# Early attention steps: the mask added on TensorE, the row minimum taken straight out of PSUM, and a new written order

## The chip, the cores and the metric

One core of a Trainium2 chip runs the whole program. Its engines are TensorE (PE, with its weight load PEld), VectorE (DVE), ScalarE (ACT) and GpSimd (POOL); all transfers are issued by SyncE (SP). Each engine has its own queue and takes its instructions in the order in which the program wrote them. The metric is the device time of one execution in microseconds (us).

## The reference

`q`, `k`, `v` have 2 batches, 8 heads, 768 positions and 64 values. For every position the scores are those against all positions, masked with -1e9 where the distance is 16 or more, and next to them the scores against 24 block maxima of `k` (blocks of 32), with log 32 added:

```
scores_l_m = where(|i - j| < 16, scale * q @ k.T, -1e9)
scores_s   = scale * q @ k_sum.T + log(32)
a = softmax(concat(scores_l_m, scores_s)); x = a @ concat(v, v_sum)
x = silu(x @ w_in) @ w_out            # 1536 x 512, inner 2048
out = (x @ w_a * (x @ w_b)) @ w_out2  # inner 1536
```

## The kernel before

**Attention.** A step is 64 query positions of one batch with all 8 heads; there are 24 (12 for each batch, numbered 0 to 23). Only a window of 96 keys can be unmasked for 64 queries, so a step scores 96 + 24 = 120 columns. Its operations are: `sc` (L349) eight score matmuls into two PSUM banks; `sm` (L370) four VectorE instructions, each of which reads 128 x 120 scores out of PSUM, adds the mask, writes the sum to SBUF and leaves its row extreme; `ex` (L389) the exponential on ScalarE; `rs` (L398) sums and reciprocal; `no` (L406) the scaling, on POOL or VectorE; `tr` (L410) four transposes into one bank; `pc` (L417) their copy to SBUF; `av` (L422) the product with the values; `xh`, `xl` (L438, L441) a part rounded to `fp32r` and the remainder. Steps in the set `ACTS` (19 of 24) have negated scores in SBUF, and ScalarE does their exponential in four instructions with the row extreme as bias, which also give the sums. The others (4, 7, 11, 19, 20) have one more operation, `su` (L384), which subtracts the extreme (on POOL), one exponential of 128 x 480 and one more sum on VectorE.

**Before attention** the keys of each batch are turned (`tk`), laid out as windows by ScalarE (`wk`), and reduced to block maxima by VectorE (`mk`, `sk`, `pk`); queries are turned (`tq`) and scaled by 1/8 (`bq`, L337); values are summed in blocks (`sv`, `mv`, `kv`).

**The two multiplications after it** are the bulk of TensorE's work. `m1:f` (12 matmuls) multiplies a block of 512 rows of x with column block f of `w_in`; `sg`, `gh`, `gl` apply the silu and split it; `m2:f` (12 matmuls) multiplies with row block f of `w_out`. Weights arrive as 64-bit words and are decoded: `da` on ScalarE, `du` and `dj` on VectorE, then split by `hi` (ScalarE or VectorE) and `lo` (POOL or VectorE). In the second and third rounds the decoded `w_out` is reloaded from DRAM (`RO`) and split again (`hR`, `lR`).

**The order** is written out by hand: `ORDER` (L26 to L77) is a list of words, and a loop (L875) calls the operation of each. A last letter is the engine: a ScalarE, v VectorE, p POOL. Each engine's queue is the list cut down to its own words; SP's is the list of loads (`LQ`, `LK`, `LG`, `LV`, `LI`, `LO`, `RO`) and spills (`SP`, `PV`). The list ends with `m2:25`; the rest of the program (from L878) is made by loops.

**PSUM.** Until the word `boot` six banks go round (L133) among `tq`, `tk`, `sc`, `mv`, `tr` and `av`; after it two. A user of a bank waits for the last reader of the user before it: for `sc` that is `sm`.

## Time and profile before

| | |
|---|---|
| median of 3 runs | 640.61 us (639.71 to 643.76) |
| the profiled execution | 643.56 us, its span 641.8 us |
| PE busy | 612.9 us, 95% of the span |
| DVE, ACT, POOL busy | 396.1, 299.7, 303.9 us |
| mean granted clock of TensorE | 0.989 of full speed |
| chain that ended last | PE 71%, DVE 4%, POOL 4%, issue 2% |

Busy time counts computing instructions; a matmul's end is modelled. Times in the rows are counted from the start of the span. The granted clock is that of TensorE as a share of its full speed. "Idle before" is the time in which the engine had nothing to do ahead of an instruction, and the name behind the arrow is what it waited for last.

### The profile page before, as it was taken

The page shows a single profiled execution, that of the slowest core. Times are in us where ns is not written, and L with a number is a line of the kernel's source. Part 1 is how long each engine was busy: PE and PEld are TensorE (multiplying, and loading weights), DVE is VectorE, ACT ScalarE, POOL GpSimd, SP SyncE. Part 2 cuts the span into 40 slices and gives each one's busy share as a digit, 9 for nine tenths or more (in the row PEclk, how much of TensorE's full clock was granted, in tenths as well). Part 3 has the DMA queues.
Part 4 walks back from the last instruction along what each step waited for, and adds up shares of the span by engine and source line. Part 5 has one row for each costly group of instructions (what it writes and reads, how often), then busy time and mean ns, then how long its engine had stood idle before and what let it go on. Part 6 is the DMA issues. An engine that isn't in the chain of part 4 may idle for free.

```text
span 641.8 us, 10139 instructions
## 1 busy us (share of the span) xinstructions
PE 612.9 (95%) x3632; PEld 528.8 (82%) x3632; DVE 396.1 (62%) x768; ACT 299.7 (47%) x651; POOL 303.9 (47%) x270
## 2 busy tenths in 40 slices
...
GB/s 231 204 177 258 283 249 308 154 203 103 62 46 58 59 37 146 229 221 195 165 199 189 116 49 73 191 104 225 83 213 83 229 16 97 84 182 302 142 2 132
DMA packets 90522, 97.82 MB, mean 152 GB/s; under 512 B 39000, under 2 KB 68440, under 8 KB 90472
## 3 DMA queue, kind: packets, MB, share of 16 engines
...
q8 instruction: 29, 0.48, 0.3%
q14 instruction: 21, 0.17, 0.1%
...
## 4 chain that ended last, share of the span: by engine, by line
PE 71%; DVE 4%; POOL 4%; issue 2%; ACT 0%; ACTq 0%; DVEq 0%; POOLq 0%
PE y L557 17%; PE h L524 15%; PE bankg L762 10%; PE bankh L762 10%; PE ol L808 10%; PE o L787 5%; POOL wab L645 1%; POOL ab L727 1%; PE av L428 1%; POOL w_out L501 1%; PE sc L358 1%; PE pt L414 1%; DVE yt L677 1%; DVE pts L148 0%; DVE sm L380 0%
## 5 line engine op out<-in xcount | busy, mean ns | idle before, releaser
L524 PE MATMUL h<-x,w_in 128*128 128x512 f32 (+1 forms) x612 | 143.0, 384 | 0.0
L557 PE MATMUL y<-g,w_out 128*128 128x512 f32 x576 | 141.3, 396 | 0.0
L524 PEld LDWEIGHTS h<-x,w_in 128*128 128x128 f32 x612 | 109.9, 190 | 22.3 <-issue 0.5
L557 PEld LDWEIGHTS y<-g,w_out 128*128 128x128 f32 x576 | 107.5, 189 | 23.9 <-issue 0.5
L501 POOL TENSOR_TENSOR w_out<-re_out,w_out 128x512 fp32r<-128x512 f32 x37 | 52.4, 1416 | 114.2 <-ACT w_out L146 108.0
L808 PE MATMUL ol<-w_out,plh 128*128 128x512 f32 x192 | 59.1, 389 | 0.0
L539 DVE TENSOR_TENSOR g<-h,g 128x512 fp32r<-128x512 f32 x31 | 21.4, 691 | 46.7 <-ACT g L146 46.5
L501 POOL TENSOR_TENSOR w_out<-w_out,w_out 128x512 fp32r<-128x512 f32 x23 | 32.0, 1402 | 34.1 <-ACT w_out L146 29.5
L539 POOL TENSOR_TENSOR g<-sg,g 128x512 fp32r<-128x512 f32 x17 | 24.8, 1461 | 43.7 <-DVE g L148 18.8
L727 POOL TENSOR_TENSOR ab<-sum,ab 128x384 f32<-128x384 f32 x24 | 27.9, 1171 | 32.2 <-DVE sum L724 32.1
L532 ACT ACTIVATE h<-h 128x512 f32<-128x512 f32 x31 | 18.1, 583 | 53.8 <-PE h L524 53.7
L808 PEld LDWEIGHTS ol<-w_out,plh 128*128 128x128 f32 x192 | 36.0, 188 | 7.5
L146 ACT CAST w_out<-re_out 128x512 fp32r<-128x512 f32 x38 | 23.6, 622 | 36.4 <-issue 27.5
L808 PE MATMUL ol<-w_out,pll 128*128 128x512 f32 x96 | 37.4, 389 | 0.0
L800 DVE TENSOR_TENSOR pll<-pl,plh 128x1024 fp32r<-128x1024 f32 x12 | 17.9, 1492 | 29.9 <-ACT plh L799 29.9
L787 PE MATMUL o<-w_out,p 128*128 128x512 f32 x108 | 30.7, 397 | 0.4 <-POOL w_out L501 0.2
L380 DVE CUSTOM_DVE_ANT_0 sm<-sc,mask 128x120 f32<-128x120 f32 x96 | 21.1, 276 | 15.5 <-PE sc L358 15.4
L393 ACT ACTIVATE sm<-sm,st 128x120 f32<-128x120 f32 x76 | 29.1, 390 | 1.5 <-DVE st L380 1.4
L478 DVE SCALAR_TENSOR_TENSOR w_out<-w_out,u_out 128x512 uint32<-128x512 uint32 x28 | 27.3, 974 | 3.0 <-ACT w_out L468 1.5
L762 PE MATMUL bankh<-yhT,wab 128*128 128x384 f32 x96 | 28.3, 335 | 0.7 <-DVE sum L709 0.7
L408 POOL TENSOR_TENSOR sm<-sm,st 128x480 f32<-128x480 f32 x20 | 22.6, 1136 | 11.7 <-DVE st L404 5.3
L501 POOL TENSOR_TENSOR w_in<-w_in,w_in 128x512 fp32r<-128x512 f32 x15 | 21.3, 1424 | 13.5 <-ACT w_in L146 7.9
...
## 6 DMA issues: line engine op xcount, KB each, us to landing
...
```

The source lines that it names most:

```text
L146: nc.scalar.copy(o, i)
L393: nc.scalar.activation(sm[:, pr, :], sm[:, pr, :], AF.Exp, scale=-1.0, bias=st[:, 0, pr:pr + 1], accum_out=st[:, 1, pr:pr + 1])
L408: engines[engine].tensor_tensor(sm, sm, st[:, 3, :, None].to_broadcast([P, NPR, KK]), op=ALU.mult)
L478: nc.vector.scalar_tensor_tensor(bits, bits, 3, u_t.pop((kind, f)), op0=ALU.logical_shift_left, op1=ALU.bitwise_or)
L501: engine.tensor_tensor(w[:, 1], w32_t[kind, f], w[:, 0].bitcast(F32), op=ALU.subtract)
L524: nc.tensor.matmul(h_ps[i][:, cols], win_t[f][:, a, c * P:(c + 1) * P], x_t[n][:, steps, m, c, :], start=(idx == 0), stop=(idx == 3 * NK - 1))
L539: engines[engine].tensor_tensor(g_t[i][:, 1], sg_t.pop(i), g_t[i][:, 0].bitcast(F32), op=ALU.subtract)
L557: nc.tensor.matmul(y_ps[n, c], wout_t[i][:, a, c * P:(c + 1) * P], g_t[i][:, m, :], start=(f == 0 and (a, m) == (0, 0)), stop=(f == N1 - 1 ...
L727: engines["v" if k == 6 else "p"].tensor_tensor(at, x, at, op=ALU.mult)
L762: nc.tensor.matmul((A, B)[b], weights(u, a, s, s + 1)[:, 0, c * P:(c + 1) * P], yc_t[q, y][m][:, c, :], start=(idx == 0 and not more), sto ...
L787: nc.tensor.matmul(o_ps[t], g[:, a, c:c + P], w[:, m], start=(begins and (a, m) == (0, 0)), stop=(ends and (a, m) == PARTS[-1]))
L808: nc.tensor.matmul(late_o[j], late_p[f][a][:, j * P:(j + 1) * P], wo2_t[N2 + f][:, m], start=(f == 0 and (a, m) == (0, 0)), stop=(f == N2 ...
```

## The change

Seven steps (`MASKED`: 0, 2, 3, 4, 5, 6, 8) get their mask from TensorE: two matmuls of 66 rows by 256 columns, one for each bank, put the mask into PSUM, and the score matmuls add to it. VectorE then takes the row minimum with two reductions out of PSUM, and ScalarE's four exponentials read PSUM. So the two banks are held until `ex`. All scores are negated when the queries are scaled, and the mask's sign is turned. POOL makes the two new operands at the start (`make_mask_product`). Steps 4, 7 and 19 now have their exponential with a bias on ScalarE; 10 and 21 have the other form, so `su` is left in 10, 11, 20 (POOL) and 21 (VectorE).

The list is written anew. Between the two lists the letters move: `no` on VectorE 4 to 13 of 24, `lo` 6 to 17 of 32, `gl` 11 to 17 of 28; the others change by one or two. Lines of the old and the new list that the prediction speaks of:

```diff
@@ -21,59 +21,61 @@
 WINDOW = 16
 NEG = -1.0e9
 
-ACTS = {0, 1, 2, 3, 5, 6, 8, 9, 10, 12, 13, 14, 15, 16, 17, 18, 21, 22, 23}
+ACTS = {0, 1, 2, 3, 4, 5, 6, 7, 8, 9, 12, 13, 14, 15, 16, 17, 18, 19, 22, 23}
+
+MASKED = {0, 2, 3, 4, 5, 6, 8}
 
 ORDER = """
-LQq:0:0 br:q:0:0:a LKq:0:0 LKq:0:1 tq:0:0:1 br:k:0:0:v ok:0 tq:0:0:0 br:k:0:1:v LKq:0:2 tk:0:0:0 mk:0:0:0 tk:0:1:1
-tk:0:0:1 tk:0:1:0 qz LQ:0:1 bq:0:0:1:a bq:0:0:0:a br:k:0:2:v tk:0:2:1 tq:0:1:0 mk:0:1:1 wk:0:0:0 wk:0:0:1 mk:0:1:0
-mk:0:2:1 tk:0:2:0 wk:0:1:1 tq:0:1:1 mk:0:0:1 mk:0:2:0 wk:0:1:0 bq:0:1:0:a LG:0:1 sk:0:v sv:0:1:1:p wk:0:2:0 pk:0:0:v
-wk:0:2:1 bq:0:1:1:v LG:0:2 sc:1 sm:1 pk:0:2:a LG:0:0 LI:1 LG:0:3 pk:0:1:v sc:0 sm:0 ex:1 sc:2 LI:0 sv:0:0:4:p LQ:0:2
-sc:5 sm:2 LV:0 sm:5 ex:0 LV:1 sv:0:3:4:v rs:1 ex:2 sv:0:2:1:p mv:0:0:512:4 no:1:p ex:5 rs:0 du:in:1 mv:0:1:0:1
-mv:0:2:0:1 mv:0:3:0:4 tr:1 sc:3 no:0:p rs:2 no:2:p tq:0:2:0 du:in:0 tr:0 sm:3 kv:0:0:a pc:1:a sc:4 sm:4 tq:0:2:1 su:4:p
-tr:2 PV:0:1 pc:0:v rs:5 ex:3 bq:0:2:0:a sc:7 av:0 LV:2 rs:3 sm:7 ex:4 av:1 no:3:p su:7:p bq:0:2:1:a PV:0:2 LV:3 rs:4
-pc:2:v da:in:1 tr:3 sc:6 no:5:p xh:0:a xh:1:a sm:6 xl:0 PV:0:3 LI:3 av:2 ex:7 tr:5 xl:1 rs:7 no:4:p pc:3:a sc:8 no:7:p
-sm:8 LV:4 ex:6 LV:5 LV:6 av:3 LV:7 rs:6 xh:2:a xh:3:a no:6:p pc:5:a LI:4 tr:4 pc:4:a da:in:0 xl:2 sc:9 ex:8 dj:in:1 xl:3
-sm:9 LI:2 hi:in:1:v av:5 tr:6 sc:11 lo:in:1:p av:4 xh:5:a pc:6:a tr:7 sm:11 pc:7:a rs:8 xl:5 sc:10 av:6 xh:4:a LV:8
-LQ:1:0 av:7 da:in:4 m1:1:0 su:11:p ok:1 no:8:p dj:in:0 xh:6:a du:in:4 xl:4 xh:7:a xl:7 hi:in:0:a LK:1:1 lo:in:0:p xl:6
...
-tk:1:2:0 hi:out:1:a hi:in:6:a sg:2:p wk:1:2:0 lo:out:0:p m1:3 da:out:2 lo:out:1:p lo:in:6:p m2:0 dj:out:2 wk:1:1:1
-gh:2:a gl:2:p du:in:5 LK:1:0 da:in:5 m2:1 LO:3 SP:2 hi:out:2:v sg:3:p dj:in:5 tk:1:0:0 m1:6 LO:4 hi:in:5:a LG:1:1
...
-du:out:5 sc:13 LO:8 hi:out:4:a hi:in:7:a gh:5:a lo:out:4:p sm:13 sc:14 gl:5:v SP:4 lo:in:7:p m1:8 hi:out:6:a da:in:9
-du:in:9 m1:7 sg:8:v da:out:5 dj:in:9 sm:14 LV:9 dj:out:5 sc:12 LO:7 hi:in:9:v lo:out:6:p du:in:10 ex:10 rs:10 LG:1:2
...
-da:out:11 gl:11:v LO:12 LV:15 sm:18 tr:12 LI:14 dj:out:10 du:out:11 lo:in:15:v pc:12:v sc:16 m1:12 sg:13:p hi:out:10:a
-dj:out:11 da:in:14 PV:1:2 PV:1:3 sm:16 av:12 xh:12:a LV:14 lo:out:10:p du:in:14 gh:13:a hi:out:11:v xl:12 SP:11 m2:10
...
-sc:22 yh:0:0 lR:17:p sm:22 yh:0:3 tr:16 yh:0:2 sg:21:p gh:18:v gl:18:v pc:16:v lR:19:v sc:21 m1:19 m2:16 gh:21:v gl:21:p
-RO:20 ex:20 sg:19:p RO:23 hR:18:v sm:21 av:18 xh:18:v xl:18 m2:17 lR:18:p tr:19 ex:22 gh:19:v hR:20:a pc:19:v ex:21
...
+LQq:0:0 LKq:0:0 ok:0 br:q:0:0:a LKq:0:1 tq:0:0:1 br:k:0:1:a br:k:0:0:v tk:0:0:0 tk:0:0:1 LKq:0:2 tq:0:0:0 tk:0:1:1
+mk:0:0:0 tk:0:1:0 LG:0:1 sv:0:1:1:p mk:0:1:1 bq:0:0:1:a wk:0:0:1 br:k:0:2:v tk:0:2:1 wk:0:0:0 mk:0:0:1 mk:0:1:0 mk:0:2:1
+wk:0:1:1 LQ:0:1 wk:0:1:0 qz tq:0:1:0 wk:0:2:1 bq:0:1:0:a LG:0:0 LG:0:2 LG:0:3 bq:0:0:0:v LI:1 LI:0 tk:0:2:0 LQ:0:2
+mk:0:2:0 sk:0:v tq:0:1:1 pk:0:1:p pk:0:2:a pk:0:0:v bq:0:1:1:v wk:0:2:0 sc:1 sm:1 sc:0 sm:0 LV:0 ex:1 sc:5 sc:2 sm:2
+ex:0 LV:1 sm:5 sv:0:3:4:v rs:1 ex:2 sv:0:0:4:p sv:0:2:1:p mv:0:0:512:4 mv:0:3:0:4 no:1:v ex:5 tr:1 rs:0 no:0:p
+mv:0:1:0:1 mv:0:2:0:1 kv:0:0:a PV:0:1 sc:3 tq:0:2:0 du:in:1 rs:2 no:2:v tr:0 pc:1:v sc:4 sm:3 da:in:1 bq:0:2:0:a du:in:0
+sm:4 pc:0:v ex:3 tq:0:2:1 tr:2 ex:4 sc:7 av:0 bq:0:2:1:a rs:3 rs:5 LV:2 av:1 no:3:p sm:7 PV:0:2 rs:4 no:4:p pc:2:a tr:3
+pc:3:a no:5:v xh:1:v xh:0:a sc:6 xl:0 sm:6 LV:3 xl:1 av:2 ex:7 LI:3 ex:6 tr:5 sc:8 rs:7 PV:0:3 LV:4 sm:8 rs:6 av:3
+xh:2:a LI:4 xh:3:a xl:2 no:7:p ex:8 tr:4 LV:5 LV:7 no:6:p pc:5:v da:in:0 sc:9 pc:4:a dj:in:1 xl:3 LV:6 LI:2 sm:9 tr:6
+av:5 pc:6:a hi:in:1:a lo:in:1:p sc:11 sm:11 su:11:p tr:7 av:4 xh:5:a av:6 rs:8 LO:0 xh:4:a xl:5 dj:in:0 pc:7:a LK:1:1
+av:7 da:in:4 hi:in:0:a m1:1:0 xh:7:a ex:11 xl:7 LQ:1:0 du:in:4 xh:6:v xl:4 no:8:v lo:in:0:p sc:10 ok:1 m1:0:0 rs:11 LV:8
...
+m1:3 sg:2:p hi:in:6:a lo:in:6:p SP:0 du:in:5 wk:1:2:0 lo:out:1:v da:out:2 m2:0 dj:out:2 LK:1:0 gh:2:a wk:1:1:1 du:in:8
+gl:2:p LO:3 sg:3:p SP:2 hi:out:2:a da:in:5 mk:1:2:0 lo:out:2:p dj:in:5 m2:1 gh:3:a hi:in:5:a m1:6 da:out:3 tk:1:0:0
...
+pk:1:0:v du:in:7 da:in:7 m2:3 dj:out:6 sc:13 m1:5 LV:11 LO:8 du:out:5 dj:in:7 gh:6:a gl:6:v hi:out:4:a LI:10 hi:in:7:a
+sm:13 sc:14 sg:5:v lo:in:7:v du:in:9 SP:4 gh:5:a gl:5:v lo:out:4:v hi:out:6:a m1:8 lo:out:6:p da:in:9 LO:7 sg:8:v
+da:out:5 LV:9 LV:10 dj:in:9 sm:14 m1:7 sc:12 hi:in:9:v du:in:10 LG:1:2 ex:10 rs:10 sm:12 dj:out:5 av:9 lo:in:9:p
...
+m1:12 du:out:11 sg:13:p dj:out:11 du:out:13 lo:in:15:p PV:1:2 dj:out:10 hi:out:10:a gh:13:a sc:16 sm:16 lo:out:10:p
+LV:14 LO:14 da:in:14 PV:1:3 av:12 SP:10 rs:15 xh:12:v du:in:14 LO:15 tr:13 xl:12 hi:out:11:a no:15:v sg:12:v pc:13:a
...
+bq:1:2:1:a SP:15 sg:16:p hi:out:15:v m1:18 RO:16 sg:18:v LV:18 rs:17 no:17:p lo:out:15:v RO:23 tr:17 first no:16:p m2:15
...
+tr:18 m1:21 yh:0:1 yh:0:2 pc:18:a sc:22 rs:19 gl:18:v hR:19:v yh:0:3 no:19:p m2:16 sm:22 tr:16 m1:19 sg:21:p pc:16:v
+gh:21:a sc:21 hR:17:a lR:17:p RO:18 m2:17 LV:19 sg:19:p gl:21:p hR:23:a sm:21 su:21:v ex:20 av:18 hR:18:a lR:18:v
...
 """
 
 
@@ -147,6 +149,9 @@
         else:
             engines[engine].tensor_copy(o, i)
 
+    def ap_of(t, offset, dims):
+        return bass.AP(tensor=t.tensor, offset=t.offset + offset, ap=[list(t.ap[0])] + dims)
+
 
     ident = const.tile([P, P], F32, name="ident")
     mask = ap1.tile([P, 3, KK], F32, name="mask")
@@ -165,16 +170,16 @@
     def make_constants():
 
         nc.gpsimd.memset(mask[:, :, 0:KL], 0.0)
-        nc.gpsimd.memset(mask[:, :, KL:KK], math.log(BLOCK))
+        nc.gpsimd.memset(mask[:, :, KL:KK], -math.log(BLOCK))
         for hp in range(2):
             m = mask[hp * QS:(hp + 1) * QS, :, 0:KL]
 
-            nc.gpsimd.affine_select(out=m, in_=m, compare_op=ALU.is_ge, fill=NEG, base=-1,
+            nc.gpsimd.affine_select(out=m, in_=m, compare_op=ALU.is_ge, fill=-NEG, base=-1,
                                     pattern=[[0, 3], [1, KL]], channel_multiplier=-1)
-            nc.gpsimd.affine_select(out=m, in_=m, compare_op=ALU.is_ge, fill=NEG, base=2 * WINDOW - 1,
+            nc.gpsimd.affine_select(out=m, in_=m, compare_op=ALU.is_ge, fill=-NEG, base=2 * WINDOW - 1,
                                     pattern=[[0, 3], [-1, KL]], channel_multiplier=1)
-        nc.gpsimd.memset(mask[:, 0, 0:WINDOW], NEG)
-        nc.gpsimd.memset(mask[:, 2, KL - WINDOW:KL], NEG)
+        nc.gpsimd.memset(mask[:, 0, 0:WINDOW], -NEG)
+        nc.gpsimd.memset(mask[:, 2, KL - WINDOW:KL], -NEG)
 
         s = sel[0:KL, KL:KK]
         nc.gpsimd.memset(sel, 0.0)
@@ -186,6 +191,27 @@
 
 
 
+    mask_r = ap1.tile([QS + 2, 3, 2 * P], F32R, name="mask_r")
+    spread_r = ap1.tile([QS + 2, P], F32R, name="spread_r")
+    log_parts = ap1.tile([QS + 2, NB], F32, name="log_parts")
+
+    def make_mask_product():
+        h = round(-math.log(BLOCK) * 1024) / 1024
+        nc.gpsimd.memset(log_parts[QS:QS + 2], h)
+
+        nc.gpsimd.affine_select(out=log_parts[QS:QS + 2], in_=log_parts[QS:QS + 2], compare_op=ALU.is_ge,
+                                fill=-math.log(BLOCK) - h, base=0, pattern=[[0, NB]], channel_multiplier=-1)
+        cols = ap_of(mask_r[0:QS], 0, [[2 * P, 3], [KK, 2], [1, KL]])
+        nc.gpsimd.memset(mask_r.bitcast(F32), 0.0)
+        nc.gpsimd.tensor_copy(cols, mask[0:QS, :, None, 0:KL].to_broadcast([QS, 3, 2, KL]))
+        nc.gpsimd.tensor_copy(ap_of(mask_r[QS:QS + 2], KL, [[2 * P, 3], [KK, 2], [1, NB]]),
+                              log_parts[QS:QS + 2, None, None, :].to_broadcast([2, 3, 2, NB]))
+        nc.gpsimd.tensor_copy(spread_r[0:QS].rearrange("p (a c) -> p a c", a=2),
+                              ident[0:QS, None, 0:QS].to_broadcast([QS, 2, QS]))
+        nc.gpsimd.memset(spread_r[QS:QS + 2].bitcast(F32), 1.0)
+
+
+
 
     qb_own = ap1.tile([P, 4, NPR, QS], F32, name="qb")
     qb = {}
@@ -194,9 +220,6 @@
 
     def window(b, j):
         return kin_t[b][:, 2 * (j // 4) + j % 4 - 1] if j % 4 in (1, 2) else kout_t[b][:, 2 * (j // 4) + j % 4 // 3]
-
-    def ap_of(t, offset, dims):
-        return bass.AP(tensor=t.tensor, offset=t.offset + offset, ap=[list(t.ap[0])] + dims)
 
     raws = [19]
 
@@ -338,9 +361,9 @@
 
         o, ps = qb[b, t][:, :, :, r::2], qt_t.pop((b, t, r))
         if engine == "v":
-            nc.vector.tensor_scalar_mul(o, ps, 1.0 / math.sqrt(D))
+            nc.vector.tensor_scalar_mul(o, ps, -1.0 / math.sqrt(D))
         else:
-            nc.scalar.activation(o, ps, AF.Copy, scale=1.0 / math.sqrt(D))
+            nc.scalar.activation(o, ps, AF.Copy, scale=-1.0 / math.sqrt(D))
 
     sm_t, pt_t, x_t = {}, {}, {}
 
@@ -350,14 +373,23 @@
 
 
         b, j = divmod(n, NJ)
-        ps = [bank(f"sc{n}")[:, 0:2 * KK].rearrange("p (a c) -> p a c", a=2) for _ in range(2)]
+        ps = [bank(f"sc{n}") for _ in range(2)]
         kw = window(b, j)
+        masked = n in MASKED
+        if masked:
+            for x in ps:
+                nc.tensor.matmul(x[:, 0:2 * P], spread_r, mask_r[:, variant(j)], start=True, stop=False,
+                                 skip_group_check=True)
+        ps = [x[:, 0:2 * KK].rearrange("p (a c) -> p a c", a=2) for x in ps]
         for pr in range(NPR):
             for hp in range(2):
                 rows, half = slice(hp * D, (hp + 1) * D), slice(pr % 2 * QS, (pr % 2 + 1) * QS)
                 nc.tensor.matmul(ps[hp][half, pr // 2, :], qb[b, j // 4][rows, j % 4, pr, :], kw[rows, pr, :],
-                                 start=True, stop=True)
+                                 start=not masked, stop=True, skip_group_check=masked)
         sc_t[n] = ps
+
+    def variant(j):
+        return 0 if j == 0 else 2 if j == NJ - 1 else 1
 
 
     st_ring = [ap1.tile([P, 4, NPR], F32, name=f"st{i}") for i in range(4)]
@@ -365,7 +397,7 @@
 
     def by_act(n):
 
-        return n in ACTS
+        return n in ACTS or n in MASKED
 
     def sm1(n):
 
@@ -374,29 +406,35 @@
         sm = ap2.tile([P, NPR, KK], F32, tag="sm", name=f"sm{n}", bufs=4)
         st = st_ring[len(st_turn) % 4]
         st_turn.append(n)
-        m = mask[:, 0 if j == 0 else 2 if j == NJ - 1 else 1, :]
-        sign, op = (-1.0, ALU.min) if by_act(n) else (1.0, ALU.max)
+        if n in MASKED:
+            for i in range(2):
+                nc.vector.tensor_reduce(st[:, 0, 2 * i:2 * i + 2], ps[i], op=ALU.min, axis=AX.X)
+            sm_t[n] = (sm, st, ps)
+            return
+        m = mask[:, variant(j), :]
+        sign, op = (1.0, ALU.min) if by_act(n) else (-1.0, ALU.max)
         for pr in range(NPR):
-            nc.vector.tensor_tensor_reduce(out=sm[:, pr, :], in0=ps[pr // 2][:, pr % 2, :], in1=m, scale=sign, scalar=-sign * 3e38,
+            nc.vector.tensor_tensor_reduce(out=sm[:, pr, :], in0=ps[pr // 2][:, pr % 2, :], in1=m, scale=sign, scalar=sign * 3e38,
                                            op0=ALU.add, op1=op, accum_out=st[:, 0, pr:pr + 1])
-        sm_t[n] = (sm, st)
+        sm_t[n] = (sm, st, None)
 
     def su(n, engine):
         if not by_act(n):
-            sm, st = sm_t[n]
+            sm, st, _ = sm_t[n]
             engines[engine].tensor_tensor(sm, sm, st[:, 0, :, None].to_broadcast([P, NPR, KK]), op=ALU.subtract)
 
     def ex(n):
-        sm, st = sm_t[n]
+        sm, st, ps = sm_t[n]
         if by_act(n):
             for pr in range(NPR):
-                nc.scalar.activation(sm[:, pr, :], sm[:, pr, :], AF.Exp, scale=-1.0, bias=st[:, 0, pr:pr + 1],
+                x = ps[pr // 2][:, pr % 2, :] if ps else sm[:, pr, :]
+                nc.scalar.activation(sm[:, pr, :], x, AF.Exp, scale=-1.0, bias=st[:, 0, pr:pr + 1],
                                      accum_out=st[:, 1, pr:pr + 1])
         else:
             nc.scalar.activation(sm, sm, AF.Exp)
 
     def rs(n):
-        sm, st = sm_t[n]
+        sm, st, _ = sm_t[n]
         if not by_act(n):
             nc.vector.tensor_reduce(st[:, 1, :], sm, op=ALU.add, axis=AX.X)
 
@@ -404,11 +442,11 @@
         nc.vector.reciprocal(st[:, 3, :], st[:, 3, :])
 
     def nm(n, engine="p"):
-        sm, st = sm_t[n]
+        sm, st, _ = sm_t[n]
         engines[engine].tensor_tensor(sm, sm, st[:, 3, :, None].to_broadcast([P, NPR, KK]), op=ALU.mult)
 
     def tr(n):
-        sm, _ = sm_t.pop(n)
+        sm = sm_t.pop(n)[0]
         ps = bank(f"pt{n}").rearrange("p (a c) -> p a c", a=NPR)
         for pr in range(NPR):
             nc.tensor.transpose(ps[0:KK, pr, :], sm[:, pr, :], ident)
@@ -814,11 +852,12 @@
     with tc.manual_schedule():
         make_first_constants()
         make_constants()
+        make_mask_product()
         for n in range(NVW):
             nc.vector.memset(vw[n][0:KL], 0.0)
             nc.vector.memset(st_ring[n][:, 2], 1e-9)
 
-        def more_blocks():
+        def more_queries():
             qb_more.append(big.tile([P, 4, NPR, QS], F32, tag="xy", name="qbm", bufs=2))
 
         def end_boot():
```

## Rows read from the trace of the kernel before

**Rows 1.** Busy us (count): PE, PEld, DVE, ACT, POOL; clock, DMA share, GB/s.
```profile
0.00:45.90 45.90, 32.70 (x437) 26.37 (x437) 30.64 (x146) 30.51 (x103) 23.72 (x42) 0.93 0.87 205
45.90:108.90 63.00, 60.47 (x403) 50.66 (x401) 53.03 (x107) 51.80 (x124) 41.25 (x33) 1.00 0.92 266
108.90:213.70 104.80, 96.70 (x674) 75.56 (x673) 62.78 (x173) 62.20 (x135) 39.05 (x31) 0.97 0.38 108
```

**Rows 2.** The same view of two stretches with a lowered clock.
```profile
20.00:30.00 10.00, 8.39 (x68) 7.06 (x67) 3.67 (x18) 6.17 (x27) 5.72 (x6) 0.66 0.92 184
...
180.00:190.00 10.00, 8.38 (x43) 6.49 (x44) 3.10 (x10) 5.59 (x8) 0.00 (x0) 0.83 0.21 48
```

**Rows 3.** Timeline of DVE, 19 to 24 us: start, us, work [idle before it, its releaser].
```profile
21.54 0.69 DVE L298 TENSOR_TENSOR vg<-vg 96x512 f32<-96x512 f32 x1 [1.57 <-DMA vg<-in_v_dram]
```

**Rows 4.** Timeline of PE, 5 to 46 us.
```profile
22.60 2.49 PE L312 MATMUL vsum<-vg,sel 96*120 96x128 f32 x10 [1.61 <-POOL vg L298]
24.88 1.06 PE L414 MATMUL pt<-ident,sm 128*120 128x128 f32 x4
```

**Rows 5.** Timeline of ACT, 7 to 47 us.
```profile
25.13 0.58 ACT L146 COPY vw<-vsum 24x512 f32<-24x512 f32 x1 [2.25 <-PE vsum L312]
...
31.89 0.60 ACT L396 ACTIVATE sm<-sm 128x480 f32<-128x480 f32 x1 [2.32 <-POOL sm L387]
```

**Rows 6.** Timeline of PE, 45.8 to 52.3 us: the first matmuls of the first multiplication.
```profile
45.89 1.70 PE L524 MATMUL h<-x,w_in 128*128 128x256 f32 x12
```

**Rows 7.** Groups by shape, 0 to 245 us: count | busy us, mean ns | idle before, releasers.
```profile
L393 ACT ACTIVATE sm<-sm,st 128x120 f32<-128x120 f32 x76 | 29.1, 390 | 1.5 <-DVE st L380 1.4
...
L408 POOL TENSOR_TENSOR sm<-sm,st 128x480 f32<-128x480 f32 x20 | 22.6, 1136 | 11.7 <-DVE st L404 5.3 <-ACT sg L532 3.1 <-PE sc L358 2.0
L501 POOL TENSOR_TENSOR w_in<-w_in,w_in 128x512 fp32r<-128x512 f32 x15 | 21.3, 1424 | 13.5 <-ACT w_in L146 7.9 <-DVE w_in L148 4.9 <-DMA st_in<-in_moe_w_in_dram 0.7
L380 DVE CUSTOM_DVE_ANT_0 sm<-sc,mask 128x120 f32<-128x120 f32 x96 | 21.1, 276 | 15.5 <-PE sc L358 15.4
L478 DVE SCALAR_TENSOR_TENSOR w_in<-w_in,u_in 128x512 uint32<-128x512 uint32 x16 | 18.4, 1159 | 3.6 <-ACT w_in L468 3.4
...
L478 DVE SCALAR_TENSOR_TENSOR w_out<-w_out,u_out 128x512 uint32<-128x512 uint32 x16 | 15.2, 952 | 1.7 <-ACT w_out L468 1.5
...
L474 DVE TENSOR_SCALAR u_out<-st_out 128x512 uint32<-128x512 uint32 x16 | 14.1, 887 | 0.0
L474 DVE TENSOR_SCALAR u_in<-st_in 128x512 uint32<-128x512 uint32 x16 | 12.9, 812 | 0.0
...
L274 DVE TENSOR_REDUCE ks<-kt 128x32 f32<-128x512 f32 x12 | 7.8, 680 | 0.7 <-PE kt L236 0.7
...
L501 DVE TENSOR_TENSOR w_out<-w_out,w_out 128x512 fp32r<-128x512 f32 x5 | 5.1, 1018 | 2.3 <-ACT w_out L146 2.3
...
L501 DVE TENSOR_TENSOR w_out<-re_out,w_out 128x512 fp32r<-128x512 f32 x7 | 4.8, 681 | 0.0
```

**Rows 8.** Timeline of DVE, 67 to 71 us: a decode shift while POOL idles.
```profile
68.91 0.43 DVE L474 TENSOR_SCALAR u_in<-st_in 128x512 uint32<-128x512 uint32 x1
```

**Rows 9.** Busy time in the first stretch of the first multiplication, columns as in 1.
```profile
45.90:67.60 21.70, 21.70 (x164) 19.93 (x162) 21.49 (x38) 18.49 (x44) 15.82 (x12) 1.00 0.94 259
```

**Rows 10.** Timeline of PE, 80 to 216 us: matmuls that waited.
```profile
84.90 1.04 PE L358 MATMUL sc<-kin,qb 64*64 64x120 f32 x16 [2.05 <-DVE st L380]
...
132.02 0.63 PE L358 MATMUL sc<-kout,qb 64*64 64x120 f32 x14 [0.83 <-DVE pts L148]
...
172.16 0.69 PE L428 MATMUL av<-pts,vw 120*64 120x64 f32 x16 [0.65 <-PE sc L358]
...
180.35 0.62 PE L414 MATMUL pt<-ident,sm 128*120 128x128 f32 x4 [0.80 <-DVE st L380]
...
182.59 0.86 PE L358 MATMUL sc<-kin,qb 64*64 64x120 f32 x14 [1.27 <-DVE pts L148]
...
191.89 0.69 PE L428 MATMUL av<-pts,vw 120*64 120x64 f32 x16 [1.44 <-issue]
```

62 lines of the change are left out of this document (30 added, 32 removed).

## Prediction

> **What bounds the kernel now.** I read the busy time by stretch first, then TensorE's own waits in it, and only then the price list. TensorE is busy for 95% of the span, so a gain can only come out of the rest. That rest lies early [rows 1]: up to 45.9 us, where the first big multiplication begins [rows 6], 13.2 us are idle; from there to 108.9 us 2.5 us; from there to 213.7 us 8.1 us. The clock takes more: 0.93 of full speed in the first stretch and 0.97 in the third. The list ends near 245 us, and behind it nothing changes. So at most some 24 us of idle time and 6 us of clock (0.07 x 45.9 + 0.03 x 104.8) are in play.
>
> In the first stretch no engine is full: VectorE works 30.6, ScalarE 30.5 of 45.9 us. It is a chain of handoffs. VectorE waits for the load of a value tile until 21.54 us, with the sums of step 1 queued behind that [rows 3]. TensorE then waits for POOL's sums of values, with the first transpose queued behind those matmuls (22.60 to 24.88 us) [rows 4]. ScalarE pays twice: 2.25 us until it can copy the sums, and 2.32 us for POOL's subtraction in step 4 [rows 5]. In the second stretch TensorE is almost full, and in its first 21.7 us VectorE is too (21.49 us) [rows 9]. In the third, all other engines have room, and what is lost are single handoffs: short attention matmuls written next to the operation whose result they need [rows 10].
>
> **The change, part by part: the mask.** Fourteen matmuls of 256 columns. The nearest row is the first multiplication's 128 x 256 form, 12 in 1.70 us, 0.142 each [rows 6]: 14 x 0.142 = 2.0 us, at half the clock 4.0. All fall before 45.9 us, where TensorE idles 13.2 us; that cover hides them, except in the chain from score to minimum, 0.28 us a step. I take 1.0 us for three to four steps on the chain; ends 0 and 4.0. POOL's new constants come at the start, where POOL's first value sum waits for its load; I take nothing, and the first keys are laid out later than that.
>
> VectorE's saving is small. One fused instruction costs 276 ns for 120 elements, a reduction out of PSUM 680 ns for 512 [rows 7]. Straight between them, 240 elements cost 0.40 us. Two reductions are 0.80 us, four fused ones at most 1.10: at most 0.30 a step, and less where the fused ones overlap. I take 0.17 x 7 = 1.2 us; ends 0 and 2.1. [...]
>
> A masked step holds its two banks until the exponentials, four of 390 ns [rows 7], end. The next users are `mv`, `tr:1` and `sc:3`, which need results of those exponentials or of POOL anyway. I take nothing beyond the chain; the upper end is 7 x (1.56 - 0.80) = 5.3 us.
>
> **Steps 4 and 7** lose POOL's subtraction and with it the wait of 2.32 us [rows 5]; ScalarE does four exponentials instead of one of 0.60 us: 2 x (1.56 - 0.60) = +1.9 us. With a key copy moved to it and some copies moved off, I take +2.6 us of ScalarE work before the first multiplication.
>
> **The early order.** On SP the last value tile is now loaded ahead of a 512 KB weight tile: at 205 GB/s [rows 1] it lands some 2.5 us earlier, and VectorE's wait of 1.57 us [rows 3] goes. The first transpose moves ahead of two matmul groups that wait for POOL, and `no:1` goes to VectorE, so ScalarE's 2.25 us go too. Against it, another value tile is loaded ahead of the second query block (384 KB, 1.9 us), and that block's turn stands in front of `sc:1` on TensorE: +0.8 us. Sum up to the first multiplication: -2.25 - 2.32 + 2.6 (ScalarE) + 1.0 (mask) + 0.8 - 1.2 (reductions) - 0.5 (`no:1`, 1.14 on POOL against 0.68 [rows 7]) = -1.9, so it begins at 44.0 us; but `sc:10` (0.6 us) is now behind that start. **Net -1.3 us**; ends -4.6 (the work is hidden) and +3.
>
> **POOL to VectorE.** Up to the first start of `m2:1`, at 67.6 us, VectorE gets 3 `lo`, 2 `no`, 1 `gl`, 1 `pc`, 1 `mk` more. Undisturbed, such an instruction costs 0.68 us [rows 7]: 8 x 0.68 = 5.4 us on an engine that was full. But POOL loses 2 `lo`, 2 `no` and 1 `gl`, 2 x 1.42 + 2 x 1.14 + 1.4 = 6.5 us, and POOL's work stretches VectorE's: the decode shift takes 0.43 us alone [rows 8] and 0.81 to 0.89 in the mean, the join 0.95 to 1.16 against 0.68 for another two-input form [rows 7]; over 64 instructions 25 us, or 0.24 us per us of POOL's 104 [rows 1]. That returns 1.6 us. About 2.4 us of VectorE's work stand behind what `m2:1` needs. So 21.49 + 5.4 - 1.6 - 2.4 = 22.9 us against TensorE's 21.7 + 0.6. I take **+0.8 us** with a handoff; ends 0 and 6.5.
>
> **Later waits.** `sc:14` waited 2.05 us behind `sc:13`; now `m1:5` stands between. VectorE is later there, so I take half, **-1.0**. `av:9` now follows `sc:12` directly; the like pair `sc:20`, `av:17` lost 0.65 [rows 10]: **+0.65**, and the same for `av:12` behind `sc:16`: **+0.65**. Filled with a big matmul are the gaps before `sc:16` (0.83), `tr:16` (0.80), `sc:21` (1.27) and `av:18` (1.44) [rows 10]: **-4.3**. With those the fall of the clock to 0.83 at 180 us [rows 2], 1.7 us, may go; half, **-0.8**. On SP the reload `RO:23` moves forward and holds a buffer while others wait; a group of 12 matmuls hides each reload, so nothing; if that fails, one wait of some 2 us.
>
> **Sum:** -1.3 + 0.8 - 1.0 + 0.65 + 0.65 - 4.3 - 0.8 = **-5.3 us**. The profiled execution took 643.56 us, 2.95 above the median of 640.61; it would become 638.3, the median **635.3 us**.
>
> **Rivals.** *A, all of it holds:* ScalarE's extra work hides in its idle 15 us, nothing new waits: -4.6 + 0.6 - 2.05 - 4.3 - 1.7 = -12: 628.6 us. For it: all these waits are handoffs, no engine is full outside one stretch. Against: two new neighbours of the same kind are in sight, and ScalarE gets more work.
>
> *B, the waits change places:* the early gain is used up by mask and held banks, and for each gap that is filled another opens: 641 us. For it: the old list, too, has big matmuls at hand and waits next to them. Against: the four late ones are filled one by one in the new list.
>
> *C, slower: VectorE becomes the bound from 45.9 to 67.6 us*, full as it is [rows 9]. A two-input instruction there costs 1.018 us when POOL works beside it [rows 7]: 8 x 1.018 - 1.6 = +6.5 us, all on TensorE's path, because `lo:out:0` and `lo:out:1` now end the chain into `m2:0`. The waits at `sc:14` and the late ones then move instead of closing: 640.6 - 1.3 + 6.5 + 1.3 = 647 us. With the later gains kept (-6.1) it decides from 0.96 us an instruction upward (8 x 0.96 = 1.6 + 6.1); without them from 0.20. Against: POOL has less to do there. [...]
>
> **How the numbers follow.** Within 1% (6.4 us) counts as no change. The forecast has 0.50, its own range 630 to 640: 0.17 of that below 634.2. A has 0.22, B 0.16 (almost all within 1%), C 0.12. Faster 0.17 + 0.22 = 0.39, taken as 0.40; same 0.33 + 0.15 = 0.48; slower 0.12. The range of 8 in 10 reaches from inside A, 627, to short of C, 644.
>
> **What would show it.** Right: the first transpose near 22.5 us, the first big matmul at 43 to 45 us, two reductions of about 0.4 us in each masked step, no wait over 0.5 us before `sc:21` and `av:18`, the list's end near 240 us. Wrong: VectorE full until 70 us with TensorE waiting for `w_out` at `m2:0` (C); the first big matmul at or past 45.9 us, with `sc` waiting for an exponential to free its bank (B); new waits of POOL or SP behind `RO:23`.

## The result, and the profile after

The changed kernel takes **632.72 us** (median of four runs, 632.34 to 633.65); the kernel before, on the same chip, 641.11 (639.71 to 643.76). The ratio is **0.9867**, with a 95% interval of 0.9832 to 0.9901. Forecast was 635.3 with a range of 627 to 644; the gain is 7.9 us against the 640.61 from which the prediction started, where it had 5.3. By the prediction's own line of 1% the kernel is faster, which had 0.40; no change had 0.48. The profiled execution took 632.82 us, its span is 631.1, its mean granted clock 1.00 (before 0.989).

Busy time by stretch of the kernel after, columns and stretches as in [rows 1], then the two stretches of [rows 2] and the first 21.7 us of [rows 9]:

```profile
0.00:45.90 45.90, 36.71 (x470) 29.57 (x471) 32.07 (x109) 35.73 (x127) 23.05 (x46) 1.00 0.99 230
45.90:108.90 63.00, 59.05 (x384) 48.41 (x383) 55.32 (x120) 46.98 (x105) 26.00 (x20) 1.00 0.88 256
108.90:213.70 104.80, 102.64 (x724) 81.35 (x723) 58.10 (x177) 69.33 (x143) 34.16 (x29) 1.00 0.40 112
...
20.00:30.00 10.00, 8.85 (x125) 7.26 (x126) 9.08 (x35) 8.83 (x40) 2.53 (x4) 1.00 0.97 206
180.00:190.00 10.00, 10.00 (x71) 7.72 (x70) 4.80 (x16) 6.52 (x10) 2.69 (x3) 1.00 0.27 72
...
45.90:67.60 21.70, 20.40 (x147) 18.20 (x146) 19.81 (x39) 14.04 (x31) 9.24 (x6) 1.00 0.80 220
```

TensorE's idle time in the three stretches was 13.2, 2.5 and 8.1 us and is 9.2, 4.0 and 2.2; the clock that was 0.66 and 0.83 is 1.00 in both. TensorE's timeline, after (start, length, work, idle before it and its releaser), answers to [rows 4, 6, 10]:

```profile
21.96 1.14 PE L335 MATMUL vsum<-vg,sel 96*120 96x128 f32 x8 [0.99 <-DVE vg L321]
23.02 0.62 PE L452 MATMUL pt<-ident,sm 128*120 128x128 f32 x4
23.84 0.48 PE L381 MATMUL sc<-mask_r,spread_r 66*128 66x256 f32 x2
...
41.83 1.68 PE L562 MATMUL h<-x,w_in 128*128 128x256 f32 x12
...
57.53 1.67 PE L562 MATMUL h<-x,w_in 128*128 128x256 f32 x12 [1.30 <-DVE g L577]
...
76.59 0.73 PE L595 MATMUL y<-g,w_out 128*128 128x512 f32 x2 [0.56 <-ACT w_out L148]
78.02 2.60 PE L595 MATMUL y<-g,w_out 128*128 128x512 f32 x10 [0.70 <-POOL w_out L539]
92.72 0.69 PE L466 MATMUL av<-pts,vw 120*64 120x64 f32 x16 [1.39 <-DVE st L417]
113.02 0.63 PE L259 MATMUL qt<-ident,raw_q 128*128 128x128 f32 x4 [0.76 <-PE sc L387]
...
131.98 0.69 PE L466 MATMUL av<-pts,vw 120*64 120x64 f32 x16 [0.65 <-PE sc L387]
...
170.00 0.69 PE L466 MATMUL av<-pts,vw 120*64 120x64 f32 x16 [0.76 <-PE sc L387]
```

Behind 45.9 us these are all its waits of over 0.3 us up to 214 us. The gaps ahead of `sc:16`, `tr:16`, `sc:21` and `av:18` [rows 10] are gone; `av:9`, `av:12` and `av:17` wait. Groups by shape up to 245 us (count | busy us, mean ns) answer to [rows 7]:

```profile
L417 DVE CUSTOM_DVE_ANT_0 sm<-sc,mask 128x120 f32<-128x120 f32 x68 | 15.0, 277 | 13.4 <-PE sc L387 10.5 <-POOL g L577 2.8
...
L512 DVE TENSOR_SCALAR u_in<-st_in 128x512 uint32<-128x512 uint32 x16 | 10.7, 676 | 0.1
...
L431 ACT ACTIVATE sm<-sc,st 128x120 f32<-128x120 f32 x28 | 9.6, 367 | 0.0
...
L512 DVE TENSOR_SCALAR u_out<-st_out 128x512 uint32<-128x512 uint32 x16 | 9.3, 580 | 2.0 <-DMA st_out<-in_moe_w_out_dram 1.8
...
L411 DVE TENSOR_REDUCE st<-sc 128x2 f32<-128x240 f32 x14 | 4.9, 399 | 2.4 <-PE sc L387 2.4
```

**Where the time came from.** I read the start of four marks on TensorE in both traces. The list's end moved by 11.4 us between the two profiled executions; the one before stood 2.5 us above its median, so about that much of the 11.4 is not in the 8.4 us by which the medians differ.

| stretch of TensorE's queue | before | after | predicted | found |
|---|---|---|---|---|
| start to first big matmul | 45.9 | 41.8 | -1.9 | -4.1 |
| from there to `m2:0` | 18.9 | 22.3 | +0.6 (`sc:10`) +0.8 | +3.4 |
| `m2:0` to `m2:7` | 44.1 | 44.6 | -0.35 | +0.5 |
| `m2:7` to the list's end | 135.9 | 124.7 | -4.45 | -11.2 |
| sum | 244.8 | 233.4 | -5.3 | -11.4 |

So in these two executions nearly all of the gain stands behind 108 us, in a part of the list that the title of the change hardly speaks of; the first 64 us end as they did before (64.8 and 64.1 us). Up to the list's end TensorE's idle time fell from 23.8 to 15.3 us (-8.5) and its busy time from 221.0 to 218.1 (-2.9), though the masks add 2.8 us (215.3 in nomask). What shortened it, the clock and score groups that a wait no longer cuts in two, is shown further down.

### The profile page after: what moved, and what is told of

Its sections match the earlier page's. It is cut to its first block, busy times and chain, and to the rows that moved or that the text cites. A ratio compares the mean times of both kernels' runs of the same rounds, so it can differ in the third digit from the quotient of the medians.

```text
span 631.1 us, 10120 instructions
## 1 busy us (share of the span) xinstructions
PE 610.1 (97%) x3646; PEld 526.0 (83%) x3646; DVE 393.1 (62%) x746; ACT 302.4 (48%) x660; POOL 275.7 (44%) x255
## 4 chain that ended last, share of the span: by engine, by line
PE 81%; DVE 5%; POOL 4%; issue 3%; ACT 3%; DMA 2%; SPq 1%; ACTq 0%; DVEq 0%; POOLq 0%
PE y L595 20%; PE h L562 18%; PE bankg L800 11%; PE bankh L800 10%; PE ol L846 10%; PE o L825 5%; PE av L466 2%; PE sc L387 2%; PE pt L452 1%; POOL wab L683 1%; POOL ab L765 1%; POOL w_out L539 1%; DMA vw<-in_v_dram 1%; DMA raw_q<-in_q_dram 1%; SPq L244 1%
## 5 line engine op out<-in xcount | busy, mean ns | idle before, releaser
L562 PEld LDWEIGHTS h<-x,w_in 128*128 128x128 f32 x612 | 108.9, 188 | 23.6 <-ACT qb L366 1.7
L539 POOL TENSOR_TENSOR w_out<-w_out,w_out 128x512 fp32r<-128x512 f32 x17 | 24.5, 1452 | 34.4 <-ACT w_out L148 29.0
L516 DVE SCALAR_TENSOR_TENSOR w_out<-w_out,u_out 128x512 uint32<-128x512 uint32 x28 | 24.0, 858 | 6.4 <-ACT w_out L506 5.1
L539 POOL TENSOR_TENSOR w_in<-w_in,w_in 128x512 fp32r<-128x512 f32 x10 | 14.5, 1455 | 28.9 <-ACT w_in L148 27.0
L743 ACT COPY sum<-bankh 128x384 f32<-128x384 f32 x12 | 5.8, 479 | 41.8 <-PE bankh L800 41.8
L577 POOL TENSOR_TENSOR g<-sg,g 128x512 fp32r<-128x512 f32 x11 | 15.2, 1383 | 21.0 <-ACT g L148 12.3
L683 POOL TENSOR_TENSOR wab<-c,wab 128x768 fp32r<-128x768 f32 x6 | 11.3, 1876 | 29.9 <-ACT wab L680 29.9
L417 DVE CUSTOM_DVE_ANT_0 sm<-sc,mask 128x120 f32<-128x120 f32 x68 | 15.0, 277 | 13.4 <-PE sc L387 10.5
```

Source lines behind the costliest of these rows:

```text
L516: nc.vector.scalar_tensor_tensor(bits, bits, 3, u_t.pop((kind, f)), op0=ALU.logical_shift_left, op1=ALU.bitwise_or)
L539: engine.tensor_tensor(w[:, 1], w32_t[kind, f], w[:, 0].bitcast(F32), op=ALU.subtract)
L562: nc.tensor.matmul(h_ps[i][:, cols], win_t[f][:, a, c * P:(c + 1) * P], x_t[n][:, steps, m, c, :], start=(idx == 0), stop=(idx == 3 * NK - 1))
L577: engines[engine].tensor_tensor(g_t[i][:, 1], sg_t.pop(i), g_t[i][:, 0].bitcast(F32), op=ALU.subtract)
L683: return lambda: engines[e].tensor_tensor(weights(u, 1, i, j), block(i + 1, j + 1), weights(u, 0, i, j).bitcast(F32), op=ALU.subtract)
```

## The experiments

Theory 1: the late order carries the gain. Theory 2, the rival: masks and early order carry it. Each ratio is to the kernel before in the same set of runs.

**nomask: no masks on TensorE.**

```diff
-MASKED = {0, 2, 3, 4, 5, 6, 8}
+MASKED = set()
```

> The changed kernel with no step masked on TensorE (the set MASKED empty): the same new order and letters, but steps 0, 2, 3, 4, 5, 6 and 8 again take the four fused VectorE instructions, and their banks are free after sm instead of after ex. Theory 1 (the new order carries the gain, the mask little): TensorE loses 14 matmuls (2.0 us), VectorE gains some 0.1 to 0.2 us a step; the first big matmul starts within 1 us of 41.8 us and the time is within 2 us of 632.7. Theory 2 (the mask carries it): the chain from score to exponential gets longer in seven steps, the first big matmul starts 2 to 4 us later and the time goes back to 636 to 640 us.

631.66 us, ratio 0.985 (0.983 to 0.9871). First big matmul at 41.0, list's end at 232.4: Theory 1. The masks win nothing: without them the kernel is at least as fast (1.1 us by the medians, though the intervals overlap).

**early_new: the new list up to `m1:1:0`, with its masks, then the old one.** **late_new: the old list up to there, no masks, then the new one.**

The first diff is early_new against the changed kernel, the second late_new.

```diff
...
-m1:1:0 xh:7:a ex:11 xl:7 LQ:1:0 du:in:4 xh:6:v xl:4 no:8:v
+sc:10 LV:8 LQ:1:0 m1:1:0 ok:1 no:8:p xh:6:a du:in:4 xl:4
...
```

```diff
-LQq:0:0 LKq:0:0 ok:0 br:q:0:0:a LKq:0:1 tq:0:0:1
+LQq:0:0 br:q:0:0:a LKq:0:0 LKq:0:1 tq:0:0:1 br:k:0:0:v
...
 m1:1:0 xh:7:a ex:11 xl:7
```

> The new list up to the first big matmul (m1:1:0), masks included, then all other words as the old list has them (steps 11, 19 and 20 with su, as before). Theory 1 (gain in the late list): the first big matmul near 42 to 43 us, but the 4 us are lost again by m2:0, where VectorE is full, and the late gaps are all there: 638 to 641 us. Theory 2 (gain from the early part and the masks): 632 to 636 us.

> The old list up to the first big matmul, no masks (steps 4, 7 and 11 with su), then all other words as the new list has them. Theory 1 (gain in the late list): the first big matmul at 45 to 47 us, no gaps over 0.8 us after 110 us, 632 to 636 us. Theory 2 (gain from the early part and the masks): 638 to 641 us, because the late list starts 4 us later.

early_new: 640.14 us, ratio 0.9981 (0.9966 to 0.9996). The first big matmul is at 41.7 us and `m2:0` even at 60.7, yet the old gaps stand where they stood (2.20 us ahead of `sc:14`, 1.27 and 1.37 us at 179 and 186 us). late_new: 634.11 us, ratio 0.9887 (0.9867 to 0.9907); first big matmul 44.5, `m2:0` 65.3, list's end 234.6, no old gap left. Against 641.41 us for the kernel before in their runs, the late list alone gives 7.3 us and the early part 1.3. By the times Theory 1 holds, but not by its path: the early 4 us are not lost by `m2:0`. In the profiled execution of early_new (638.40 us, 1.7 below its median) the transpose that waits at 206.26 us before the change comes at 200.73, so there they are not spent at all. Against that, the four executions of early_new with a mean clock of 0.997 take 638.40 to 640.17 us, and four of the kernel before at 0.997, over all sets, 637.19 to 638.96. So where the early 4 us go stays open; by the medians they are worth 1.3.

**before_fill: the kernel before with four words moved**, so that a big group stands in each of the four late gaps.

```diff
-sc:16 m1:12
+m1:12 sc:16
...
-sc:22 yh:0:0
+sc:22 m2:16 yh:0:0
...
-sc:21 m1:19 m2:16
+m1:19 sc:21
...
-sm:21 av:18 xh:18:v xl:18 m2:17
+sm:21 m2:17 av:18 xh:18:v xl:18
```

> The kernel before with four words of its list moved and nothing else: the first product's group m1:12 ahead of sc:16, m2:16 directly after sc:22, m1:19 ahead of sc:21, m2:17 ahead of av:18. Theory 1 (TensorE's gaps late in the list are what the new order closes): the four gaps of 0.83 to 1.44 us go and the clock holds at 180 to 190 us, list's end near 240 in place of 244.8, time 636 to 637. Rival (the waits change places, because VectorE and ScalarE are late anyway): new gaps of the same size behind the moved words, 640 to 642. If Theory 1 holds only in part, the rest of the late gain is in the split of the work between POOL, VectorE and ScalarE.

635.91 us, ratio 0.9932 (0.9907 to 0.9956): **-4.6 us** from 640.55. The four gaps are gone; one of 0.65 us stands ahead of `av:12`, as the prediction had it for the new list, and one of 0.45 at 188.7 us. The windows of this run (columns as above), between 115 and 120 and between 180 and 190 us:

```profile
115.00:120.00 5.00, 5.00 (x21) 4.00 (x21) 4.93 (x5) 2.61 (x6) 5.00 (x4) 0.81 0.68 190
...
180.00:190.00 10.00, 9.55 (x85) 7.33 (x84) 5.08 (x17) 6.99 (x21) 3.45 (x3) 1.00 0.31 74
```

With the gaps the clock's fall at 180 us went too (0.83 in [rows 2], here 1.00); the fall at 115 us, where nothing was moved, stayed. The prediction had 4.3 + 0.8 for just this step, less 0.65 at `av:12`.

**pool_back: the changed kernel with 24 `lo` and `no` back on POOL.**

```diff
-no:1:v
+no:1:p
...
-lo:out:0:v
+lo:out:0:p
...
-lo:out:13:v
+lo:out:13:p
...
```

> The changed kernel with the letters of lo and no put back to POOL where the old list had POOL (24 instructions), in the new order. Theory 1 (moving them to VectorE pays, because POOL's work stretches VectorE's and takes twice as long): POOL's busy time rises by some 30 us, the decode shift and join on VectorE go back to means of 0.8 to 1.2 us, and the time rises by 2 to 6 us, to 635 to 639 us. Theory 2 (the moves make VectorE the bound between 46 and 68 us): the first m2 starts earlier than 64 us and the time falls to 629 to 632 us.

644.08 us, ratio 1.0048 (1.0029 to 1.0068): 11 us lost, more than either theory had. Up to 146.5 us its marks are nearly those of the changed kernel; then TensorE waits in `m2:12`, and ScalarE ahead of the decode `da:out:15`:

```profile
153.29 4.64 PE L595 MATMUL y<-g,w_out 128*128 128x512 f32 x10 [6.13 <-POOL w_out L539]
```

```profile
149.51 0.66 ACT L506 ACTIVATE w_out<-st_out 128x512 f32<-128x512 f32 x1 [5.33 <-DMA sp_out<-w_out]
```

The splits `lo` on POOL, in the changed kernel and then here:

```profile
143.29 1.58 POOL L539 TENSOR_TENSOR w_out<-w_out,w_out 128x512 fp32r<-128x512 f32 x1 [4.47 <-PE av L466]
```

```profile
150.75 2.48 POOL L539 TENSOR_TENSOR w_out<-w_out,w_out 128x512 fp32r<-128x512 f32 x2 [5.86 <-ACT w_out L148]
```

POOL is not full there: it, too, sits idle, for 5.86 us. What holds it is its queue. By the list, the row of the changed kernel is `lo:out:12`, the split that `m2:12` needs. Here the two are `lo:out:14` and `lo:out:12`, in this order, since `lo:out:14` is one of the 24 that went back to POOL. `lo:out:14` needs ScalarE's `hi:out:14`, which stands in ScalarE's queue behind `da:out:15`, and that waits for a buffer that is still being spilled. So a split that TensorE wants stands behind one that isn't ready; in the changed kernel `lo:out:14` is on VectorE, and `lo:out:12` runs 8 us earlier. Behind the wait TensorE is slow, too: the ten matmuls of `m2:12` take 4.64 us, where all twelve take 2.88 in the changed kernel, and the score group that follows takes 1.08 (0.64); from 108.9 to 213.7 us the clock is 0.97, 1.00 in the changed kernel. And transposes wait 3.0 us for `no` on POOL. Those 11 us therefore say little on what VectorE's work costs beside POOL's.

**before_mask: the masks of the seven steps in the old order.**

```diff
+MASKED = {0, 2, 3, 4, 5, 6, 8}
...
-sm:4 su:4:p
+sm:4
```

> The kernel before with the masks of the same seven steps added by TensorE and the minimum taken out of PSUM, in the old order (the one word su:4 is gone, since step 4 then goes by ScalarE). Theory 1 (the order carries the gain, the masks by themselves little): 640 to 642, first big matmul 45 to 46 us after the start. Rival (the masks carry the early part): first big matmul at 42 to 43, clock 1.00 between 20 and 30 us, time 637 to 639. A third way, that PSUM banks held until the exponentials stop TensorE in the old order: 643 or more.

644.02 us, ratio 1.0044 (1.0012 to 1.0076): slower. First big matmul at 47.8 us; from 0 to 45.9 us the clock was 0.81. The time lies in the range of the third way, and its mechanism shows once: `av:5`, the next user of a bank of step 8, waits 1.04 us for an exponential.

```profile
42.45 0.69 PE L466 MATMUL av<-pts,vw 120*64 120x64 f32 x16 [1.04 <-ACT sm L431]
```

No matmul of a score group waits so, and neither the kernel before nor the changed kernel has such a wait. The other part that shows is the clock: its six executions go from 640.12 us at a mean clock of 0.997 to 645.75 at 0.980.

**mix: the changed kernel with the old words between the first big matmul and `m2:0`.** **mix_nomask: the same without masks.**

```diff
-m1:1:0 xh:7:a ex:11 xl:7 LQ:1:0 du:in:4 xh:6:v xl:4 no:8:v
+sc:10 LV:8 LQ:1:0 m1:1:0 ok:1 no:8:p xh:6:a du:in:4 xl:4
...
-wk:1:2:0 lo:out:1:v da:out:2 m2:0
+wk:1:2:0 lo:out:0:p m1:3 da:out:2 lo:out:1:p lo:in:6:p m2:0
```

> The changed kernel, but from the first big matmul to the first group of the second product (m2:0) in the old order; from there on its own list. In the changed kernel TensorE spends 22.3 us between these two points, 20.5 of them busy, with 1.30 us of wait for VectorE's gelu product; with the old words there (the run with early part new, rest old) 19.0 us, all busy. Theory 1 (that stretch loses 1.8 us to VectorE by its order, and 1.5 us are only work that stands later): the wait goes, time 630 to 631.5, list's end 231.5 to 232.5. Rival (VectorE has as much to do as the stretch is long, so what it is spared here it lacks further on): the wait comes back before m2:3 or av:9, time 632 to 634.

> The mix of before (the changed kernel, with the old words between the first big matmul and m2:0) with no step masked by TensorE: the reductions of those seven steps add the mask from SBUF as in the kernel before. Theory 1 (the masks cost TensorE more than they spare VectorE, in this order as in the changed kernel, where leaving them out gave 1 us): 628.5 to 629.3. Rival (with TensorE no longer waiting for VectorE from 42 to 61 us, VectorE's saving shows or the lowered clock costs it): 629.8 to 631.

mix: **629.83 us**, ratio 0.9835 (0.9808 to 0.9862), just below the range of Theory 1; mix_nomask: **629.19 us**, ratio 0.9818 (0.9783 to 0.9854), as its Theory 1 has it. Every execution of either (630.35 at most) is below every one of the changed kernel (632.34 at least), though the intervals of the ratios overlap. The stretch from the first big matmul to `m2:0` in the changed kernel, and then in mix:

```profile
41.80:64.10 22.30, 20.48 (x169) 18.32 (x166) 21.22 (x42) 16.16 (x39) 8.92 (x9) 1.00 0.83 213
```

```profile
41.90:61.00 19.10, 19.10 (x154) 17.64 (x150) 18.39 (x37) 16.91 (x39) 14.85 (x14) 1.00 0.88 237
```

In the changed kernel VectorE is busy for 21.2 of 22.3 us and TensorE waits 1.8; in mix POOL does 14.9 us of work where it did 8.9, and TensorE is never idle. The list's end comes at 230.9 us in place of 233.4: of the 3.1 us that `m2:0` gains, 2.5 arrive. The old words bring both their order and their letters, so mix doesn't tell these two apart. The masks' price in this order, 0.64 us, is inside the runs' spread.

**av9: `m2:4` directly behind `sc:12`, ahead of `av:9`.**

```diff
-sc:12 hi:in:9:v
+sc:12 m2:4 hi:in:9:v
...
-no:10:p m2:4 da:in:10
+no:10:p da:in:10
```

> The changed kernel with one word moved: m2:4 directly after sc:12, so ahead of av:9 instead of behind m2:4's old place. In the changed kernel av:9 waits 1.39 us for VectorE's row of statistics behind sc:12. Theory 1 (a gap of TensorE ahead of the list's end costs its own length when a group stands ready): wait gone, 631.2 to 631.8, list's end 232 from 233.4. Rival (m2:4 itself waits there for its weights or for g, or the next wait grows by as much): 632.5 to 633.

632.25 us, ratio 0.9878 (0.985 to 0.9906). The wait of 1.39 us is gone; 1.12 us ahead of a group of the first product (`g`, at 105.3 us) have come. The query turn at 114 us waits 1.35 in place of 0.76, but it does so in late_vg (1.41) and mix (1.16) too, where this word was not moved. The time lies between the two forecasts; the rival's mechanism is right here: most of this wait changed its place.

**late_vg: the load `LI:1` ahead of `LG:0:3`, as before.**

```diff
-LG:0:2 LG:0:3 bq:0:0:0:v LI:1
+LG:0:2 LI:1 LG:0:3 bq:0:0:0:v
```

> The changed kernel with one load put back: LI:1 ahead of LG:0:3 on SyncE's queue, as in the kernel before, so that the last rows of the first batch's values come 0.5 to 1 us later. Theory 1 (the early order's gain comes from these loads: VectorE's sum over them, then vsum, then the first transpose, is the chain): vsum's wait longer by 0.5 to 1 us, first transpose 23.6 to 24 us (23.02 in the changed kernel), time 633 to 633.7. Rival (the early gain is the reductions' and the exponentials' order, the loads are beside it): first transpose 23.0 to 23.2, 632.4 to 632.9.

632.66 us, ratio 0.9872 (0.9829 to 0.9914); `vsum` waits 1.06 us (0.99), the first transpose is at 23.05: the rival's numbers. Nothing hangs on this load.

**late_lg1: the values' first load and POOL's sums over it put back behind the queries.** **fill_lg: before_fill with that load moved forward.**

```diff
-tk:0:1:0 LG:0:1 sv:0:1:1:p mk:0:1:1
+tk:0:1:0 mk:0:1:1
...
-bq:0:1:0:a LG:0:0
+bq:0:1:0:a LG:0:1 sv:0:1:1:p LG:0:0
```

```diff
-tk:0:1:0 qz
+tk:0:1:0 LG:0:1 sv:0:1:1:p qz
...
-bq:0:1:0:a LG:0:1 sk:0:v sv:0:1:1:p
+bq:0:1:0:a sk:0:v
```

> The changed kernel with the first load of the values (LG:0:1) and POOL's sums over it put back behind the blocks of queries, as they stood in the kernel before: in the changed kernel that load is issued at 5.03 us, before the change at 8.83. Theory 1 (the early gain is this load: POOL's sums begin at 12.5 us in place of 15.2, and TensorE's wait for them falls from 3.1 to 1.0 us): POOL's sums from about 15 us, vsum's waits 2.5 to 3 us, first transpose 24 to 25 us, first big matmul 43.5 to 45, time 634 to 635.5. Rival (the early gain is in the order of the steps, and POOL catches up before its sums are wanted, or what is lost is taken up before the list's end): first transpose 23 to 23.5, 632.4 to 633.2.

> The kernel before with the four late words moved (635.91 in an earlier run) and two more: the first load of the values LG:0:1 and POOL's sums over it ahead of the first turns of queries, as in the changed kernel. No masks by TensorE, no other change of order or of engines. Theory 1 (this load makes the early gain, by shorter waits for POOL's sums and by the clock): vsum's waits fall from 3.1 us to near 1, clock 0.98 or more up to 45.9 us, first big matmul 42.5 to 44.5, time 632 to 634. Rival (the load works only together with the rest of the early order, since the blocks of queries then come 1.9 us later and with them sc:1): first big matmul 45.5 or later, 635 to 637.

late_lg1: 636.23 us, ratio 0.9898 (0.9847 to 0.9949), above both ranges; its executions go from 633.45 us at a mean clock of 0.999 to 637.64 at 0.989. In the profiled one, the slowest, the first big matmul is at 46.3 us. Its timeline of TensorE, the window from 20 to 30 us, and that window in fill_lg:

```profile
22.77 4.18 PE L335 MATMUL vsum<-vg,sel 96*120 96x128 f32 x16
26.75 1.06 PE L452 MATMUL pt<-ident,sm 128*120 128x128 f32 x4
```

```profile
20.00:30.00 10.00, 9.94 (x78) 8.39 (x78) 5.58 (x17) 5.45 (x26) 2.79 (x4) 0.52 0.71 150
```

```profile
20.00:30.00 10.00, 9.32 (x71) 7.68 (x72) 5.73 (x41) 7.58 (x35) 5.04 (x6) 0.66 0.96 197
```

TensorE hardly waits between 20 and 30 us here (9.94 us busy), it is slow: the clock is 0.52, and four transposes take 1.06 us, 0.62 in the changed kernel. fill_lg: 635.58 us, ratio 0.992 (0.9892 to 0.9949), first big matmul at 45.6, clock 0.66 as in [rows 2]. So the rival of fill_lg is right: the early load alone does not bring the early gain.

Over all profiles of this case, one execution of each kernel, the window from 20 to 30 us has two kinds: with the new early order and its load the clock there is 1.00 (the changed kernel, nomask, early_new, pool_back, mix, mix_nomask, av9, late_vg), without either of them 0.52 to 0.66 (before, before_fill, before_mask, late_new, late_lg1, fill_lg). But the order does not fix the clock. One execution of late_lg1 had a mean clock of 0.999 and took 633.45 us, no more than the changed kernel's slowest (633.65), and one of fill_lg had 1.000 and took 633.37. So that the load is needed is not shown; with the new order and its load the fall came between 20 and 30 us in none of the eight profiles, without them in all six.

## Why the prediction was right or wrong

The result lies in the range, on the side of the forecast's sign, between it and rival A. The mechanisms were mostly right; the late term and the stretch ahead of `m2:0` were too small, the second of them cancelled with the early part, which was luck, and one reading was wrong.

**Late gaps and clock: the mis-sized term.** The prediction fills the gaps before `sc:16`, `tr:16`, `sc:21` and `av:18` for -4.3 us and takes half of the clock, -0.8. For those four that was right: before_fill gives 4.6 us. But from `m2:7` on 11.2 us went. Idle time there fell from 8.1 to 2.2 us, 5.9 in place of 3.65 (4.3 less 0.65 at `av:12`): I took from the trace only the gaps that I had recognised in the list. TensorE's timeline of the kernel before, at a place that I left out, and the last of these groups in the changed kernel:

```profile
113.07 0.63 PE L358 MATMUL sc<-kout,qb 64*64 64x120 f32 x14 [0.82 <-DVE x L442]
114.34 0.86 PE L236 MATMUL qt<-ident,raw_q 128*128 128x128 f32 x4 [0.64 <-PE sc L358]
...
116.19 3.85 PE L557 MATMUL y<-g,w_out 128*128 128x512 f32 x12
```

```profile
114.19 3.02 PE L595 MATMUL y<-g,w_out 128*128 128x512 f32 x12
```

Of these 1.46 us of waiting 0.76 are left, and the group of twelve behind them, 3.85 us, takes 3.02 after the change. The same matmuls from `m2:7` to the list's end kept TensorE busy for 5.3 us less. The clock explains at most 3.4 of it: 5 us each at 0.96, 0.70, 0.79 and 0.87 (at 110, 115, 180 and 185 us), (0.04 + 0.30 + 0.21 + 0.13) x 5. Another part is the score matmuls, 144 in both kernels: they kept TensorE busy for 7.63 us before and 5.77 after. A score group that waited for its second bank was cut in two, and the pieces took longer than the whole, 0.42 and 0.63 us against 0.64. `sc:16`, before and after:

```profile
130.78 0.42 PE L358 MATMUL sc<-kout,qb 64*64 64x120 f32 x2
132.02 0.63 PE L358 MATMUL sc<-kout,qb 64*64 64x120 f32 x14 [0.83 <-DVE pts L148]
```

```profile
130.69 0.64 PE L387 MATMUL sc<-kout,qb 64*64 64x120 f32 x16
```

So that gap cost 0.41 us more than its idle time, and the one ahead of 113.07 us, cut in two like it (0.42 and 0.63 us), as much. How much of the gain is the clock's can be seen in another way, too: four executions of the kernel before with a mean clock of 0.997 took 637.19 to 638.96 us, and the one of the changed kernel at 0.997 took 633.65. At one clock 3.5 to 5.3 us of the 8.4 are left.

**The early part: too small, for the wrong reason.** I had the first big matmul at 44.0 us; it came at 41.8. ScalarE's two waits went as I had it: of 2.25 us for the sums 0.9 are left, and of the 2.32 us in step 4 nothing. But that the last value tile "lands some 2.5 us earlier, and VectorE's wait of 1.57 us" goes was a misreading: VectorE begins that sum at 21.23 us (21.54 before), merely with other work ahead of it, and late_vg shows that the load past which it moved is of no account. What else moved is `LG:0:1` (issued at 5.03 us, before at 8.83) and the order of the steps around it: with them TensorE is busy for 14.3 of the first 20 us (11.9 before), and the clock of 0.66 that followed from 20 to 30 us, which I had named as in play and left out of the sum, is 1.00. That is at most 0.34 x 10 = 3.4 us. late_lg1, where it is 0.52 in the profile, loses 2.0 us by the ratios, whose intervals overlap, and 3.5 by the medians. In the time little of it arrives: early_new gains 1.3 us.

**VectorE ahead of `m2:0`: +0.8 was too small.** The stretch is 3.4 us longer. 1.6 us is busy time: the only group that is new in it is `sc:10`, and that takes 1.05 us in two pieces, where I had 0.6; the rest is not traced. The other 1.8 us is idle: 1.30 for VectorE's `g` and 0.52 inside `sc:10`, for which the profile names no releaser. mix takes the idle time away, and most of it arrives at the end. So rival C's mechanism, a VectorE that is full (21.2 of 22.3 us), is there at a quarter of its price, but not on the path that C named: `m2:0` does not wait for `lo:out:0` or `lo:out:1`. The two early errors cancelled by luck: I had -0.5 up to `m2:0`, it was -0.7.

**VectorE's price beside POOL** I took as a slope: so many us for each us of POOL's work. As one number that does not hold. In pool_back POOL is busy for 111.8 us of the first 245 (88.7 in the changed kernel, 113.5 before), and yet the shifts `u_in` take 688 ns and `u_out` 568, as in the changed kernel (676 and 580) and not as before (812 and 887) [rows 7]. The joins go both ways: that of `w_out` takes 912 ns (750 in the changed kernel, 952 before), that of `w_in` 938 (994, 1159 before). A single overlap does show the price. One join, `dj:out:12`, in the changed kernel, where POOL idles, and in pool_back, where POOL runs a split:

```profile
141.98 0.68 DVE L516 SCALAR_TENSOR_TENSOR w_out<-w_out,u_out 128x512 uint32<-128x512 uint32 x1
```

```profile
142.17 1.58 DVE L516 SCALAR_TENSOR_TENSOR w_out<-w_out,u_out 128x512 uint32<-128x512 uint32 x1
```

```profile
141.92 1.28 POOL L539 TENSOR_TENSOR w_out<-w_out,w_out 128x512 fp32r<-128x512 f32 x1 [4.14 <-ACT w_out L148]
```

So what counts seems to be which instructions meet, not how much POOL has; no run isolates it further.

**The masks: the cost nearly right, the sign of the net not.** The 14 matmuls add 2.8 us to TensorE's busy time up to the list's end (218.1 against 215.3 us in nomask; I had 2.0). A reduction took 399 ns; I had 0.40. In the first step that has it, two of them take 0.72 us:

```profile
17.95 0.72 DVE L411 TENSOR_REDUCE st<-sc 128x2 f32<-128x240 f32 x2
```

The four fused instructions just ahead of them, for step 1, take 0.89 us from the first start (17.05) to the last end, so a step saves the 0.17 us that I took. But no run shows a gain: without masks both good orders are 1.1 and 0.6 us faster by the medians (inside the spread), and in the old order the masks cost 3.5 us by the medians; at a mean clock of 0.997 it is 640.12 against 637.19 to 638.96. The held bank, which I had put at nothing beyond the chain, made TensorE wait 1.04 us there. So the masks win nothing, but VectorE's reductions are not where they lose.

**The rest.** `sc:14`'s wait is gone (2.05; I took half). `av:9` waits 1.39 us (0.65 predicted) and `av:12` 0.65 (0.65). `m2:3` waits 1.26 us for its weights, which I had not foreseen. Nothing waits behind `RO:23`. Rival B, waits that change place, shows in av9, where 1.12 of 1.39 us came back.
